# Attention scores from operands loaded early, two heads on two halves of the rows, sums by TensorE in the first 16 steps

## The chip, the cores and the metric

One Trainium2 chip, one of its cores. The metric is the device time of one execution in microseconds, the median of the runs. One execution was also taken with the hardware profiler; all rows below are from it.

## The reference

Three layers in a row, all float32. Attention: 4 batches, 8 heads, 576 positions, 64 dimensions a head.

```python
scores = scale * np.matmul(q, k.transpose(0, 1, 3, 2))        # scale = 1/8
bias = slopes[:, None, None] * (-np.abs(rel))[None, :, :]     # slopes 2^-(h+1), rel = pos_q - pos_k
mask = (rel >= 0) & (rel < 128)
scores = np.where(mask, scores + bias[None], -1e9)
attn = np.exp(scores - np.max(scores, axis=-1, keepdims=True))
attn = attn / (np.sum(attn, axis=-1, keepdims=True) + 1e-9)
x = np.matmul(attn, v)                                        # then (tokens 2304) x (512)
x = (np.maximum(x @ w_in, 0) ** 2) @ w_out                    # 512 -> 2048 -> 512
h = x @ w_in2; x = (h * np.cos(h)) @ w_out2                   # 512 -> 2048 -> 512
```

## The kernel before

**Tiling.** The 2304 tokens (the four batches, one behind the other) are 18 blocks `j` of 128 queries. A step `a` is one block and one of its four pairs of heads (`j, hp = divmod(a, 4)`; `e` is the head within the pair), so there are 72 steps. A query block needs its own keys and those of the block before it (`slot` says where each lies); the first block of each two batches needs only its own ("first"), block 4 of nine straddles two batches ("straddle", with a bias table of its own), the one behind it ("after") uses 192 columns.

**A step** is: `scores` (products of queries and keys into a PSUM bank, then for each head the bias and the row minimum of -score/8 in one VectorE instruction, line 386, and the exponential with its row sum on ScalarE, line 396), `normalise` (row sum plus 1e-9, reciprocal, and the scaling of the exponentials, lines 408, 409, 412), `transposes` (four TensorE transposes into a bank of `ps_s`, one ScalarE copy back, line 423) and `values` (products with V, line 449, of two heads into two halves of the columns; done for the four steps of a block together by `values_of_block`). With the fourth pair the block's output goes from PSUM to the next layer's operand as a high and a low part, `xh` (ScalarE, line 463) and `xl` (VectorE, line 464).

**Scores of the first seven blocks** (`PLAIN = 7`, steps 0 to 27) are full float32 products (line 354). Their operands are "planes" `s0_j` in the places of the weight tiles 9 to 15 (`S0`), 512 KB each in HBM: for each pair of heads, queries of head 0, a middle part with the keys of both heads, queries of head 1. The unused half of each query part is zeroed by POOL (lines 320, 321), so a product runs over all 128 rows and the zeros take the other head out. Later blocks use split operands (`QH`, `QL`, `KS`, line 365). A float32 product is two TensorE instructions in the trace.

**Two phases.** Steps 0 to 15 (`START = 16`) run ahead of the dense layers; their score banks are the four `ps_y` banks. Then the main loop runs over units of the dense layers (`h_mms`: 12 products of 512 columns, `y_mms`: 12 more), and one or two attention steps are put into each: scores of step s+1, `h_mms`, transposes of step s, `y_mms`. Their score banks come from `ps_s`, two banks, which the transposes use as well.

**Weights** come in 1 MB tiles, two loads ahead at most, and each is turned into a high and a low part by jobs (`w_top` ScalarE line 185 after a POOL memset, `w_rest` VectorE line 189, `w_split` ScalarE line 201 and VectorE line 204). `tick` advances the jobs. In the first phase two are started (`START_W`); tiles 9 to 15 wait for the planes in their places.

**Order.** Loads go to SP's queue (some of the first to ScalarE's) in written order: a load that waits for its buffer keeps those behind it waiting. `load_v(j + 2)` stands at the end of a block's values, and there are three V buffers; `load_plain(j + 2)` stands in `scores` of the block's second pair. On the other engines the framework makes one stream for each engine from the written order and its own estimate of when operands are ready, so conversions and steps interleave otherwise than they are written.

Of the kernel before, what the change touches and what calls it, by code (L numbers as in the profile page):

```python
# [8 lines left out]
F32 = mybir.dt.float32  # L9
F32R = mybir.dt.float32r  # L10
BF16 = mybir.dt.bfloat16
# [3 lines left out]
AF = mybir.ActivationFunctionType  # L15
ALU = mybir.AluOpType
# [6 lines left out]
P = 128  # L23
# [30 lines left out]

START, LOOK, PLAIN = 16, 2, 7


A_OPEN, W_OPEN, START_W = 20, 1, 2  # L60

SEAT = NF - PLAIN

# [10 lines left out]


@with_exitstack
def attention_mlp_mlp(ctx: ExitStack, tc: tile.TileContext, kq, s0, v, w1, w2, bias, strad, ident, out):

# [174 lines left out]
    def slot(j):  # L253

        return (j + j // 9) % 2
# [41 lines left out]
        )  # L297


    Pt, St, Tt, Oacc = {}, {}, {}, {}  # L300

    def kind(j):
        return {0: "first", 4: "straddle", 5: "after"}.get(j % 9, "plain")
# [2 lines left out]
        return {"first": (0, 128), "after": (64, 256)}.get(kind(j), (0, 256))  # L306

    def load_v(j, queue=sp):
        if j < NJ:
            V[j] = vp.tile([P, H * D], F32, tag="v", name=f"v_{j}")  # L310
            queue.dma_start(V[j], v[j])

    def load_plain(j, hps=slice(0, 4)):


        if j >= PLAIN:
            return
        t = plain(j)
        if hps.start == 0:
            pool.memset(t[64:128, :, 0], 0.0)  # L320
            pool.memset(t[0:64, :, 2], 0.0)
        for e in range(2):
            rows = slice(64 * e, 64 * e + 64)
            sp.dma_start(t[rows, hps, e : e + 2], s0[j][rows, hps])

    S0 = [wp.tile([P, 2048], F32, tag=f"w{SEAT + j}", name=f"s0_{j}") for j in range(PLAIN)]

    def plain(j):
        return S0[j][:, 0:1536].rearrange("p (a c t) -> p a c t", a=4, c=3)

    def scores_to(a):
        while now["qk"] < min(a, STEPS - 1):
            scores(now["qk"] + 1)

    def scores(a):

        j, hp = divmod(a, 4)
        if j >= PLAIN:
            if j == PLAIN:
                run_until(("kq", j - 1, hp))  # L340
            run_until(("kq", j, hp))
        now["qk"] = a
        if hp == 1:
            load_plain(j + 2)
            if j == 2:
                sp.dma_start(strad_sb, strad)
        if a < START:
            sbank = ps_y.tile([P, 2, 256], F32, tag=f"y{a % 4}", name=f"s_{a}")
# [13 lines left out]
        for i, src in enumerate((QH, QL)) if j >= PLAIN else ():  # L362
            for e in range(2):
                h = 2 * hp + e
                te.matmul(  # L365
                    sbank[:, e, :],
                    src[j, hp][:, e, :],
                    KS[:, :, h, :],
                    start=(i == 0 and e == 0),
                    stop=(i == 1),  # L370
                    skip_group_check=True,
                )
        if a < START:
            pt = S0[a % PLAIN][:, 1536:2048].rearrange("p (e c) -> p e c", e=2)
        else:
            pt = pp.tile([P, 2, 256], F32, tag="p", name=f"p_{a}")
        st = stp.tile([P, 8], F32, tag="st", name=f"st_{a}")
        Pt[a], St[a] = pt, st
        kd = kind(j)
        b0 = 0 if slot(j) else 128  # L380
        c0, c1 = cols(j)
        if kd == "after":
            pool.memset(pt[:, :, 0:64], 0.0)
        for e in range(2):
            h = 2 * hp + e
            dve.tensor_tensor_reduce(  # L386
                out=sbank[:, e, c0:c1],
                in0=sbank[:, e, c0:c1],
                in1=strad_sb[:, h] if kd == "straddle" else bias_sb[:, h, b0 + c0 : b0 + c1],
                scale=-0.125,  # L390
                scalar=3.0e38,
                op0=ALU.add,
                op1=ALU.min,
                accum_out=st[:, e : e + 1],
            )
            act.activation(  # L396
                pt[:, e, c0:c1],
                sbank[:, e, c0:c1],
                AF.Exp,
                bias=st[:, e : e + 1],  # L400
                scale=-1.0,
                accum_out=st[:, 2 + e : 3 + e],
            )
# [32 lines left out]
    def values(s):  # L436
        now["v"] = s
        j, hp = divmod(s, 4)
        ns = 1 if kind(j) == "first" else 2
        ptT = Tt.pop(s)  # L440
        if hp == 0:
            Oacc[0] = ps_o.tile([P, 4, P], F32, tag="o", name=f"o_{j}")
        ob = Oacc[0]
        for c in range(ns):

            blk = j if ns == 1 or c == slot(j) else j - 1
            for e in range(2):
                h = 2 * hp + e
                te.matmul(  # L449
                    ob[64 * e : 64 * e + 64, hp, :],  # L450
                    V[blk][:, h * D : h * D + D],
                    ptT[:, e, c, :],
                    start=(hp == 0 and c == 0),
                    stop=(c == ns - 1),
                    skip_group_check=True,
                )
# [148 lines left out]
    with ExitStack():  # L605
# [12 lines left out]
        dve.memset(halfpi, math.pi / 2)  # L618
        load_plain(0, slice(0, 1))
        act.dma_start(bias_sb[:, 0:2], bias[:, 0:2])  # L620
        load_plain(0, slice(1, 4))
# [136 lines left out]
```

## Time and profile before

| | |
|---|---|
| time, median of 3 runs | 936.79 us (935.21 to 937.61) |
| the profiled execution | 934.74 us, its span 933.0 us |
| mean granted TensorE clock | 0.996 of 2.4 GHz |
| busy: TensorE, VectorE, ScalarE | 911.6, 580.2, 502.8 us |
| moved by DMA | 70.36 MB |

The span runs from the first to the last instruction of the execution. An engine's busy time is what its instructions cover; the ends of TensorE's are modelled. In a timeline row with "x8", eight instructions are merged, and the first two numbers are the start and the length of the whole.

### The profile page before, as it was taken

The page shows a single profiled execution, that of the slowest core. Times are in us where ns is not written, and L with a number is a line of the kernel's source. Part 1 is how long each engine was busy: PE and PEld are TensorE (multiplying, and loading weights), DVE is VectorE, ACT ScalarE, POOL GpSimd, SP SyncE. Part 2 cuts the span into 40 slices and gives each one's busy share as a digit, 9 for nine tenths or more (in the row PEclk, how much of TensorE's full clock was granted, in tenths as well). Part 3 has the DMA queues.
Part 4 walks back from the last instruction along what each step waited for, and adds up shares of the span by engine and source line. Part 5 has one row for each costly group of instructions (what it writes and reads, how often), then busy time and mean ns, then how long its engine had stood idle before and what let it go on. Part 6 is the DMA issues. An engine that isn't in the chain of part 4 may idle for free.

```text
span 933.0 us, 13113 instructions
## 1 busy us (share of the span) xinstructions
PE 911.6 (98%) x5040; PEld 772.4 (83%) x5040; DVE 580.2 (62%) x1283; ACT 502.8 (54%) x1014; POOL 39.6 (4%) x58
## 2 busy tenths in 40 slices
PE   5699999999999999999999999999999999999998
PEld 5588888888888888888888888888888888888898
DVE  4969557666666566654645687566556555655554
ACT  5879656555555545554545575454444444444443
POOL 3112000000000000000110100000000000000000
PEclk9999999999999999999999999999999999999999
DMA  9773221311112111125234360011001000100010
GB/s 271 195 309 135 99 102 46 102 69 46 58 57 91 58 46 46 48 100 179 93 129 144 113 202 24 1 46 46 1 0 46 1 1 1 45 1 1 1 46 23
DMA packets 28846, 70.36 MB, mean 75 GB/s; under 512 B 2800, under 2 KB 11888, under 8 KB 28784
## 3 DMA queue, kind: packets, MB, share of 16 engines
q1 hardware_dynamic: 27920, 68.16, 21.8%
q10 hardware_dynamic: 864, 1.38, 0.6%
q8 instruction: 39, 0.64, 0.3%
q14 instruction: 23, 0.19, 0.1%
HBM read 60.09 MB, written 9.44 MB: 75 GB/s over the span
## 4 chain that ended last, share of the span: by engine, by line
PE 91%; ACT 4%; DVE 2%; DMA 2%; issue 1%; SPq 0%; POOL 0%; ACTq 0%; DVEq 0%
PE y L552 14%; PE y L554 13%; PE y L553 13%; PE h L493 13%; PE h L494 13%; PE h L495 13%; PE o L449 3%; PE t L421 3%; PE s L365 2%; PE s L354 2%; DMA s<-s_in 1%; ACT cv_w L185 1%; DVE cv_w L189 0%; ACT s L396 0%; ACT w L201 0%
## 5 line engine op out<-in xcount | busy, mean ns | idle before, releaser
L493 PE MATMUL h<-xh,w 128*128 128x512 f32 (+1 forms) x640 | 237.2, 371 | 0.0
L494 PE MATMUL h<-xl,w 128*128 128x512 f32 (+1 forms) x640 | 236.1, 369 | 0.0
L495 PE MATMUL h<-xh,w 128*128 128x512 f32 (+1 forms) x640 | 235.6, 368 | 0.0
L495 PEld LDWEIGHTS h<-xh,w 128*128 128x128 f32 x640 | 120.6, 188 | 20.4
L493 PEld LDWEIGHTS h<-xh,w 128*128 128x128 f32 x640 | 120.8, 189 | 19.4 <-ACT ysb L567 0.2
L494 PEld LDWEIGHTS h<-xl,w 128*128 128x128 f32 x640 | 120.9, 189 | 18.5
L552 PE MATMUL y<-rh,w 128*128 128x512 f32 (+1 forms) x320 | 123.4, 387 | 0.4 <-DVE ysb L567 0.4
L554 PE MATMUL y<-rh,w 128*128 128x512 f32 (+1 forms) x320 | 118.4, 370 | 0.0
L553 PE MATMUL y<-rl,w 128*128 128x512 f32 (+1 forms) x320 | 118.2, 370 | 0.0
L552 PE MATMUL y<-gh,w 128*128 128x512 f32 (+1 forms) x320 | 117.8, 369 | 0.2 <-ACT gh L532 0.2
L553 PE MATMUL y<-gl,w 128*128 128x512 f32 (+1 forms) x320 | 117.7, 368 | 0.0
L554 PE MATMUL y<-gh,w 128*128 128x512 f32 (+1 forms) x320 | 117.7, 368 | 0.0
L522 ACT ACTIVATE r<-r 128x512 f32<-128x512 f32 x72 | 45.5, 632 | 120.4 <-DVE r L521 120.4
L533 DVE TENSOR_TENSOR gl<-r,gh 128x512 fp32r<-128x512 f32 x72 | 49.8, 692 | 75.9 <-ACT gh L532 75.9
L519 DVE SCALAR_TENSOR_TENSOR r<-kk,h 128x512 f32<-128x512 int32 x72 | 49.5, 687 | 63.5 <-ACT kk L518 63.4
L510 DVE TENSOR_TENSOR a<-a 128x512 f32<-128x512 f32 x62 | 42.9, 692 | 62.9 <-ACT rh L509 59.9
L499 ACT ACTIVATE a<-h 128x512 f32<-128x512 f32 x72 | 43.0, 597 | 71.7 <-PE h L495 70.7
L396 ACT ACTIVATE p<-s,st 128x256 f32<-128x256 f32 (+2 forms) x112 | 51.5, 460 | 54.5 <-DVE st L386 54.4
L518 ACT ACTIVATE kk<-h 128x512 int32<-128x512 f32 x72 | 42.9, 596 | 69.3 <-PE h L495 69.2
L386 DVE CUSTOM_DVE_ANT_0 s<-s,bias_sb 128x256 f32<-128x256 f32 (+2 forms) x128 | 51.5, 407 | 38.6 <-PE s L354 13.9
L554 PEld LDWEIGHTS y<-rh,w 128*128 128x128 f32 x320 | 60.3, 188 | 10.7
L552 PEld LDWEIGHTS y<-rh,w 128*128 128x128 f32 x320 | 60.4, 189 | 10.4 <-issue 1.7
(69 smaller groups left out, 1377.0 us busy)
## 6 DMA issues: line engine op xcount, KB each, us to landing
raw<-w_in SPq DMA_DIRECT2D x32, 1023.8 KB, 6.9
raw_a<-kq_in SPq DMA_DIRECT2D x44, 256.0 KB, 2.6
y<-ysb SPq DMA_DIRECT2D x18, 256.0 KB, 2.1
raw_a<-y SPq DMA_DIRECT2D x18, 256.0 KB, 2.6
v<-v_in SPq DMA_DIRECT2D x16, 256.0 KB, 2.7
out<-ysb SPq DMA_DIRECT2D x16, 256.0 KB, 2.4
s<-s_in SPq DMA_DIRECT2D x12, 256.0 KB, 7.9
v<-v_in ACTq DMA_DIRECT2D x2, 256.0 KB, 6.5
```

Of the source, the lines that this page charges most:

```text
L386: dve.tensor_tensor_reduce(out=sbank[:, e, c0:c1], in0=sbank[:, e, c0:c1], in1=strad_sb[:, h] if kd == "straddle" else bias_sb[:, h, b0 + ...
L396: act.activation(pt[:, e, c0:c1], sbank[:, e, c0:c1], AF.Exp, bias=st[:, e : e + 1], scale=-1.0, accum_out=st[:, 2 + e : 3 + e],)
L493: te.matmul(o, wh[:, cs], xh, start=(c == 0 and kt == 0), stop=False, skip_group_check=True)
L494: te.matmul(o, wh[:, cs], xl, start=False, stop=False, skip_group_check=True)
L495: te.matmul(o, wl[:, cs], xh, start=False, stop=(kt == KT - 1), skip_group_check=True)
L499: act.activation(Aa[i], Hb.pop(i), AF.Relu)
L519: dve.scalar_tensor_tensor(r, kk, -C1, hb, ALU.mult, ALU.add)
L522: act.activation(r, r, AF.Abs)
L533: dve.tensor_tensor(rl, r, rh.bitcast(F32), ALU.subtract)
L552: te.matmul(o, wh, gh, start=(first and not (two and m % 2)), stop=False, skip_group_check=True)
L553: te.matmul(o, wh, gl, start=False, stop=False, skip_group_check=True)
L554: te.matmul(o, wl, gh, start=False, stop=last, skip_group_check=True)
```

## The change

Planes hold queries and keys of both heads of a pair, head 0 on rows 0 to 63 and head 1 on rows 64 to 127, with no zeros (1024 columns, one contiguous load for each plane). A score product runs over 64 rows, the two heads alternate, and each head has its own bank: in steps 0 to 15 two steps are made together and share two `ps_y` banks, in steps 16 to 27 one step takes half of both `ps_s` banks. The queues get all planes and V 0 to 2 ahead of the first step, with weight tiles 0 and 1 between them. One table of 640 bf16 columns is loaded in place of the bias tables (768 and 512 KB), and VectorE scales it for each head. In steps 0 to 15 the exponentials are not normalised and have no row sums: TensorE also multiplies the transposed exponentials with a tile of ones, into the `ps_h` bank, and the block's output is multiplied with the reciprocal of these sums. An exponential on a constant stands ahead of everything on ScalarE. Left out of the diff: the removed constants and argument, the packing of planes and tables on the host, and `kq` steps from 28 on, which stay as they were.

```diff
+    ones = cst.tile([P, D], F32, name="ones")
+    warm = cst.tile([P, 1], F32, name="warm")
+    dve.memset(halfpi, math.pi / 2)
+    dve.memset(ones, 1.0)
+    act.activation(warm, halfpi, AF.Exp)
...
     def top_up():
         for c in "aw":
-            if now["qk"] < {"a": A_OPEN, "w": W_OPEN}[c]:
+            if c == "a" and now["qk"] < A_OPEN:
...
     def load_v(j, queue=sp):
-        if j < NJ:
+        if j < NJ and j not in V:
...
-    def load_plain(j, hps=slice(0, 4)):
-        if j >= PLAIN:
-            return
-        t = plain(j)
-        if hps.start == 0:
-            pool.memset(t[64:128, :, 0], 0.0)
-            pool.memset(t[0:64, :, 2], 0.0)
-        for e in range(2):
-            rows = slice(64 * e, 64 * e + 64)
-            sp.dma_start(t[rows, hps, e : e + 2], s0[j][rows, hps])
+    def load_plain(j, hps=slice(0, 4), queue=sp):
+        queue.dma_start(plain(j)[:, :, hps], s0[j][:, :, hps])
...
+    def make_bias(dst, src, heads):
+        for h in heads:
+            dve.tensor_scalar(dst[:, h], src, 2.0**-h, None, ALU.mult)

     def scores_to(a):
         while now["qk"] < min(a, STEPS - 1):
-            scores(now["qk"] + 1)
+            a0 = now["qk"] + 1
+            steps = (a0, a0 + 1) if a0 < START else (a0,)
+            if a0 == START // 2:
+                make_bias(strad_sb, base_sb[:, 384:640], range(H))
+            scores(steps)
+            exps(steps)
...
+        if len(steps) == 2:
+            k = steps[0] // 2 % 2
+            banks = [ps_y.tile([P, 2, 256], F32, tag=f"y{2 * k + e}", name=f"s_{steps[0]}_{e}") for e in range(2)]
         else:
-            sbank = ps_s.tile([P, 2, 256], F32, tag="s", name=f"s_{a}")
-        if j < PLAIN:
-            for e in range(2):
-                for b in (j,) if kind(j) == "first" else (j, j - 1):
+            banks = [ps_s.tile([P, 2, 256], F32, tag="s", name=f"s_{steps[0]}_{e}") for e in range(2)]
+        for i, a in enumerate(steps):
+            Sc[a] = [bank[:, i] for bank in banks]
+            for b in (j,) if kind(j) == "first" else (j, j - 1):
+                for e in range(2):
+                    rows = slice(64 * e, 64 * e + 64)
                     te.matmul(
-                        sbank[:, e, slot(b) * P : slot(b) * P + P],
-                        plain(j)[:, hp, 2 * e],
-                        plain(b)[:, hp, 1],
-                        start=(e == 0 and b == j),
+                        Sc[a][e][:, slot(b) * P : slot(b) * P + P],
+                        plain(j)[rows, 0, a % 4],
+                        plain(b)[rows, 1, a % 4],
+                        start=(i == 0 and b == j),
...
+    def exps(steps):   # per head: the bias and row minimum of all steps, then their exponentials
...
+                    accum_out=St[a][:, 2 + e : 3 + e] if a >= START else None,
...   (values)
+            if s < START:
+                Oacc[1] = ps_h.tile([P, 4, P], F32, tag="h", name=f"sum_{j}")
...
+            products = [(ob, lambda h: V[blk][:, h * D : h * D + D])]
+            if s < START:
+                products.append((Oacc[1], lambda h: ones))
...
+            if s < START:
+                total = gp.tile([P, 4, P], F32, tag="a", name=f"total_{j}")
+                x = gp.tile([P, 4, P], F32, tag="a", name=f"x_{j}")
+                dve.tensor_scalar(total, Oacc[1], 1e-9, None, ALU.add)
+                dve.reciprocal(total, total)
+                dve.tensor_tensor(x, ob, total, ALU.mult)
+                ob = x
             act.copy(xh[:, :, ts], ob)
...
+        base_sb = rp.tile([P, 1024], BF16, tag="a", name="base_sb")
+        load_plain(0, slice(0, 2))
+        act.dma_start(base_sb[:, 0:640], bias)
+        make_bias(bias_sb, base_sb[:, 0:384], range(2))
+        load_plain(0, slice(2, 4))
         act.dma_start(id_sb, ident)
         load_v(0, act)
-        act.dma_start(bias_sb[:, 2:4], bias[:, 2:4])
-        act.dma_start(bias_sb[:, 4:8], bias[:, 4:8])
+        make_bias(bias_sb, base_sb[:, 0:384], range(2, H))
         load_plain(1)
-        load_v(1, act)
-
-        scores_to(0)
-        for s in range(START):
-            scores_to(min(s + LOOK, START))
+        AHEAD["w"] = 1
+        top_up()
+        load_plain(2)
+        load_v(1)
+        AHEAD["w"] = 2
+        top_up()
+        load_plain(3)
+        load_v(2)
+        for j in range(4, PLAIN):
+            load_plain(j)
+
+        scores_to(1)
+        for s in range(0, START, 2):
+            scores_to(min(s + 3, START))
             values_of_block()
-            normalise(s)
-            transposes(s)
-            tick("aw" if s < START_W else "a")
+            for a in (s, s + 1):
+                transposes(a)
+                tick("aw" if a < START_W else "a")
```

## Rows read from the trace of the kernel before

**Rows 1.** The page, busy time, share of the span and instructions of each engine.
```profile
PE 911.6 (98%) x5040; PEld 772.4 (83%) x5040; DVE 580.2 (62%) x1283; ACT 502.8 (54%) x1014; POOL 39.6 (4%) x58
```

**Rows 2.** Windows: length, busy time of each engine, granted clock, DMA share, GB/s.
```profile
0.00:5.20 5.20, 0.00 (x0) 0.02 (x1) 0.06 (x1) 0.00 (x0) 4.40 (x12) 1.00 0.57 159
5.20:9.90 4.70, 1.20 (x5) 0.95 (x5) 0.36 (x2) 1.74 (x3) 4.32 (x8) 1.00 1.08 224
9.90:41.60 31.70, 26.01 (x229) 22.52 (x229) 27.59 (x118) 27.74 (x77) 2.45 (x4) 1.00 0.89 250
41.60:46.30 4.70, 1.75 (x12) 1.14 (x12) 4.70 (x14) 2.97 (x11) 1.90 (x2) 0.70 0.89 202
46.30:53.50 7.20, 7.08 (x52) 6.00 (x53) 3.56 (x16) 3.28 (x8) 0.00 (x0) 0.72 0.36 124
53.50:132.50 79.00, 78.91 (x456) 66.13 (x454) 56.05 (x132) 59.33 (x119) 10.36 (x14) 1.00 0.42 157
```

**Rows 3.** The chain that ended last, 0 to 56 us: start, length, what.
```profile
2.65 7.11 DMA s<-s_in
...
41.64 0.53 SPq L324
42.22 4.13 DMA s<-s_in
```

**Rows 4.** Waits of SP's queue, 0 to 54 us: total, times, longest.
```profile
SPq L311 <- PE o L449: 24.6, 3, 9.7
```

**Rows 5.** Windows of lines 408, 409 and 412 alone: busy time, instructions.
```profile
0.00:53.50 53.50, 2.81 (x17) 0.94 0.80 218
0.00:53.50 53.50, 2.47 (x17) 0.94 0.80 218
0.00:53.50 53.50, 10.47 (x34) 0.94 0.80 218
```

**Rows 6.** Groups by form on VectorE: busy time, mean ns, idle before.
```profile
L521 DVE TENSOR_SCALAR r<-r 128x512 f32<-128x512 f32 x72 | 30.7, 426 | 2.1
...
L464 DVE TENSOR_TENSOR xl<-o,xh 128x512 fp32r<-128x512 f32 x18 | 12.4, 688 | 6.7 <-ACT xh L463 6.5
...
L409 DVE RECIPROCAL st<-st 128x2 f32<-128x2 f32 x72 | 11.6, 164 | 2.0
```

**Rows 7.** Timeline of ScalarE, two exponentials and a reading: start, length.
```profile
26.28 0.47 ACT L396 ACTIVATE s<-s,st 128x256 f32<-128x256 f32 x1
26.64 0.20 ACT L396 ACTIVATION_READ_ACCUMULATOR s<-s,st 128x1 f32 x1
26.73 0.47 ACT L396 ACTIVATE s<-s,st 128x256 f32<-128x256 f32 x1
```

**Rows 8.** A step's scores in the chain, a block's values in the timeline.
```profile
85.53 0.89 PE s L354 x8
...
81.67 2.28 PE L449 MATMUL o<-p,v 128*64 128x128 f32 x32
```

**Rows 9.** Groups by form, TensorE's weight loads of 128 and 64 columns.
```profile
L421 PEld LDWEIGHTS t<-id_sb,p 128*128 128x128 f32 x216 | 27.0, 140 | 7.1
L449 PEld LDWEIGHTS o<-p,v 128*64 128x64 f32 x432 | 23.3, 137 | 5.4 <-issue 5.1 <-ACT p L423 0.3
```

**Rows 10.** Timelines: three transposes and the next step's first exponential.
```profile
53.84 0.60 PE L421 MATMUL t<-id_sb,p 128*128 128x128 f32 x4
54.96 0.48 ACT L396 ACTIVATE p<-s,st 128x256 f32<-128x256 f32 x1
...
79.75 0.60 PE L421 MATMUL t<-id_sb,p 128*128 128x128 f32 x4
80.04 0.44 ACT L396 ACTIVATE p<-s,st 128x192 f32<-128x192 f32 x1
...
89.00 0.60 PE L421 MATMUL t<-id_sb,p 128*128 128x128 f32 x4
89.61 0.43 ACT L396 ACTIVATE p<-s,st 128x192 f32<-128x192 f32 x1
```

More of the change, by code (lines that the diff above doesn't have):

```diff
@@ L76, in attention_mlp_mlp @@
 @with_exitstack
-def attention_mlp_mlp(ctx: ExitStack, tc: tile.TileContext, kq, s0, v, w1, w2, bias, strad, ident, out):
+def attention_mlp_mlp(ctx: ExitStack, tc: tile.TileContext, kq, s0, v, w1, w2, bias, ident, out):
     nc = tc.nc
@@ L341, in scores @@
             run_until(("kq", j, hp))
[L342 to L348, printed above, removed]
-        else:
-            sbank = ps_s.tile([P, 2, 256], F32, tag="s", name=f"s_{a}")
-        if j < PLAIN:
-            for e in range(2):
-                for b in (j,) if kind(j) == "first" else (j, j - 1):
+            sbank = ps_s.tile([P, 2, 256], F32, tag="s", name=f"s_{a}")
+            Sc[a] = [sbank[:, e] for e in range(2)]
+            for i, src in enumerate((QH, QL)):
+                for e in range(2):
+                    te.matmul(
+                        Sc[a][e],
+                        src[j, hp][:, e, :],
+                        KS[:, :, 2 * hp + e, :],
+                        start=(i == 0 and e == 0),
+                        stop=(i == 1),
+                        skip_group_check=True,
+                    )
+            return
+        if len(steps) == 2:
+            k = steps[0] // 2 % 2
+            banks = [ps_y.tile([P, 2, 256], F32, tag=f"y{2 * k + e}", name=f"s_{steps[0]}_{e}") for e in range(2)]
+        else:
+            banks = [ps_s.tile([P, 2, 256], F32, tag="s", name=f"s_{steps[0]}_{e}") for e in range(2)]
+        for i, a in enumerate(steps):
+            Sc[a] = [bank[:, i] for bank in banks]
+            for b in (j,) if kind(j) == "first" else (j, j - 1):
+                for e in range(2):
+                    rows = slice(64 * e, 64 * e + 64)
                     te.matmul(
-                        sbank[:, e, slot(b) * P : slot(b) * P + P],
-                        plain(j)[:, hp, 2 * e],
-                        plain(b)[:, hp, 1],
-                        start=(e == 0 and b == j),
+                        Sc[a][e][:, slot(b) * P : slot(b) * P + P],
+                        plain(j)[rows, 0, a % 4],
+                        plain(b)[rows, 1, a % 4],
+                        start=(i == 0 and b == j),
                         stop=True,
@@ L361, in scores @@
                     )
[L362 to L378, printed above, removed]
+    def exps(steps):
+        j = steps[0] // 4
         kd = kind(j)
@@ L381, in scores @@
         c0, c1 = cols(j)
-        if kd == "after":
-            pool.memset(pt[:, :, 0:64], 0.0)
-        for e in range(2):
[L385 to L403, printed above, removed]
+        for a in steps:
+            if a < START:
+                k = a % (2 * PLAIN)
+                pt = S0[k // 2][:, 1024 + k % 2 * 512 : 1536 + k % 2 * 512].rearrange("p (e c) -> p e c", e=2)
+            else:
+                pt = pp.tile([P, 2, 256], F32, tag="p", name=f"p_{a}")
+            Pt[a], St[a] = pt, stp.tile([P, 8], F32, tag="st", name=f"st_{a}")
+            if kd == "after":
+                pool.memset(pt[:, :, 0:64], 0.0)
+        for e in range(2):
+            for a in steps:
+                h = 2 * (a % 4) + e
+                dve.tensor_tensor_reduce(
+                    out=Sc[a][e][:, c0:c1],
+                    in0=Sc[a][e][:, c0:c1],
+                    in1=strad_sb[:, h] if kd == "straddle" else bias_sb[:, h, b0 + c0 : b0 + c1],
+                    scale=-0.125,
+                    scalar=3.0e38,
+                    op0=ALU.add,
+                    op1=ALU.min,
+                    accum_out=St[a][:, e : e + 1],
+                )
+            for a in steps:
+                act.activation(
+                    Pt[a][:, e, c0:c1],
+                    Sc[a][e][:, c0:c1],
+                    AF.Exp,
+                    bias=St[a][:, e : e + 1],
+                    scale=-1.0,
+                    accum_out=St[a][:, 2 + e : 3 + e] if a >= START else None,
+                )
     def normalise(a):
@@ L446, in values @@
             blk = j if ns == 1 or c == slot(j) else j - 1
[L447 to L456, printed above, removed]
+            products = [(ob, lambda h: V[blk][:, h * D : h * D + D])]
+            if s < START:
+                products.append((Oacc[1], lambda h: ones))
+            for bank, stationary in products:
+                for e in range(2):
+                    te.matmul(
+                        bank[64 * e : 64 * e + 64, hp, :],
+                        stationary(2 * hp + e),
+                        ptT[:, e, c, :],
+                        start=(hp == 0 and c == 0),
+                        stop=(c == ns - 1),
+                        skip_group_check=True,
+                    )
         if hp == 3:
@@ L721, in bias_table @@
         c = np.arange(P)[None, :]
-        t = np.empty((P, H, 384), np.float32)
-        for h in range(H):
-            slope = 2.0 ** -(h + 1)
-            prev = np.where(c > r, -8.0 * slope * (P + r - c), -8.0e9)
-            cur = np.where(c <= r, -8.0 * slope * (r - c), -8.0e9)
-            t[:, h] = np.concatenate([prev, cur, prev], axis=1)
-        return t.astype(ml_dtypes.bfloat16)
-    def straddle_table():
-        t = bias_table()[:, :, 128:].copy()
-        t[64:, :, :64] = -8.0e9
-        t[64:, :, 128:] = -8.0e9
-        return t
+        out = -8.0e9 * 2.0 ** (H - 1)
+        prev = np.where(c > r, -4.0 * (P + r - c), out)
+        cur = np.where(c <= r, -4.0 * (r - c), out)
+        ends = np.where((r >= 64) & (c < 64), out, cur), np.where(r >= 64, out, prev)
+        return np.concatenate([prev, cur, prev, *ends], axis=1).astype(ml_dtypes.bfloat16)
     arrays = {
```

25 lines of the change are left out of this document (11 added, 14 removed).

## Prediction

> **What bounds the kernel now.** I read the page's busy shares first. TensorE is busy 98% of the span [rows 1], so a gain can only come from its 2% of gaps or from TensorE work that goes away. The busy times by stretch show where the gaps are [rows 2]: from 53.5 to 132.5 us TensorE is busy 78.91 of 79.00 us, so everything behind 53.5 us is bound by TensorE's own work. Ahead of 53.5 us it isn't. Of 5.2 to 9.9 us TensorE works 1.20 us and VectorE 0.36. From 9.9 to 41.6 us three engines are nearly level: ScalarE 27.74, VectorE 27.59, TensorE 26.01 of 31.70 us. From 41.6 to 46.3 us TensorE works 1.75 of 4.70 us. In the two stretches from 41.6 to 53.5 us the granted clock averages 0.70 and 0.72, so about half of each ran at 1.2 GHz and not at 2.4: it fell after TensorE had begun to stand.
>
> The chain of waits names the two holes [rows 3]. The first is the load of the rest of plane 0, in flight from 2.65 to 9.76 us. The second is the load of plane 4: SP issues it only at 41.64 us and TensorE waits for it until 46.35. The waits of SP's queue say why it is issued late [rows 4]: the load of V blocks (line 311) waits 24.6 us in three waits, up to 9.7 us each, for the value products that free its buffer, and plane 4's load stands behind one of them.
>
> **Early loads.** All seven planes and V 0 to 2 go to the queues ahead of the first step, before any load that waits for a buffer, so the 41.6 us hole has no cause left. That is worth up to 4.7 us. VectorE was busy through the whole hole [rows 2], but partly with conversions of weight tiles 2 and 3, which can go behind 53.5 us, where VectorE is idle 79.0 - 56.05 = 23 us; I take 3.5. The cold stretch behind it (46.3 to 53.5 us) held TensorE 7.08 us at a mean clock of 0.72; at the full clock the same work is about 7.08 x 0.72 = 5.1 us, 2.0 less. Together -5.5 us (bounds -2, if VectorE binds there after all, and -6.7). What is late next is the load of V 3, which waits for V 0's buffer and is needed in block 3 only. In SP's queue weight tile 0 now stands between planes 1 and 2, and tile 1 between 2 and 3; the 1.0 MB of tile 0 and the 0.52 MB each of planes 1 and 2 are, at the 250 GB/s of [rows 2], 2.1 MB or 8.4 us behind plane 0, so about 15 us, when block 2 is not yet on; all of it (planes, tiles 0 and 1, V 1 and 2: 5.7 MB) is there 23 us behind plane 0, at about 29 us, and step 16 needs plane 4 at about 40.
>
> At the start 5.2 us x 159 GB/s + 4.7 us x 224 GB/s = 1.9 MB had come in when the rest of plane 0 was there [rows 2]. Now steps 0 to 3 need plane 0 (0.52 MB), a table of 0.16 MB in place of 0.77 MB of bias, the identity (0.07) and V 0 (0.26): 1.0 MB, which those rates bring by 5.2 + (1.0 - 0.83) / 0.224 = 6.0 us. So the hole shrinks from 4.7 us to about 1.2: -3.5 us (bounds 0, if the table, which now leaves ScalarE's queue behind the warm-up exponential, is as late as plane 0 was; and -4.7). The memsets of the planes on POOL go; they were ahead of need.
>
> **VectorE and ScalarE in the first 16 steps.** The normalising by rows (lines 408, 409, 412) cost 2.81 + 2.47 + 10.47 = 15.75 us for 17 steps [rows 5]; step 16 keeps it, so 14.8 go. Added for each of four blocks are a sum with 1e-9, a reciprocal and a product, each 128x512. The sum and the product read PSUM like the xl subtraction, 0.69 us [rows 6]. No 128x512 reciprocal is in the trace: one pass like the scalar operation of that shape is 0.43 us; the 128x2 form took 0.164 us, at most 82 ns a column if nothing of it were fixed, which gives 42 us for 512. Between ends so far apart I take the nearest 128x512 row, 0.69; the range keeps 0.43 and, above, eight passes (4.4, among the rivals), and leaves 42 out. So 4 x 2.07 = 8.3 us come. The tables cost 16 scalings of 384 or 256 columns; by the 512-column row at most 0.43 us each, at least 0.16 like the 2-column one; I take 0.3, 4.8 us. VectorE: -14.8 + 8.3 + 4.8 = -1.7 us. ScalarE loses the reading of the row sums: an exponential takes 0.36 us from its start to the reading's, and 0.09 more until the next one starts [rows 7]: 32 x 0.09 = -2.9 us.
>
> The Trainium skill, "VectorE: DVE Perf Modes", section "First, the fixed hardware budget", says that a reciprocal runs iterative divide operations with a repeat count of 8. The two-column row cannot show it; by that rule the sum here would be 9 us worse, which is the second rival below.
>
> **TensorE in the first 16 steps.** Scores cost 0.89 us a step of two blocks [rows 8], so eight instructions of 0.111 us. Two heads on different halves of the rows are not in the trace. The nearest row is the value products, which stand on two halves of the columns: 32 in 2.28 us, 0.071 each [rows 8]. Bounds are 0.111 (no overlap; a little above that if switching costs) and half of it, 0.055. I take 0.071, so 0.57 a step, and 0.32 saved. For 4 half steps and 12 whole ones that is 14 x 0.32 = -4.5 us. The sums by TensorE double the value products: 4 x 0.29 + 12 x 0.57 = +8.0 us. TensorE's net is +3.5 us.
>
> In the stretch from 9.9 to 41.6 us this makes TensorE 29.5, VectorE 26 and ScalarE 25 of 31.7 us: two engines lighter, the third heavier but below the length. I take 0 for its length (bounds -3, as ScalarE's saving, and +5, TensorE's extra work and the dependences of pairs). At the end of the phase the sum, the reciprocal and the product stand in a row ahead of xh: 3 x 0.69 = 2.1 us, which only the scores and transposes of steps 16 and 17 can cover: +1.5 us (0 to +2.1).
>
> The Trainium skill, "TensorE: Matmul & The Clock Gate", section "LDWEIGHTS (loading the stationary operand)", says that a weight load takes as long as it has columns, however few rows. The trace agrees on columns [rows 9]: 23.3 / 432 = 0.054 us busy per load of 64 columns, 27.0 / 216 = 0.125 of 128. If loads alone set the pace, scores gain nothing; that is the third rival. The same page's "Measured speedup vs the span model" has row tiles run side by side, by which they would halve.
>
> **Behind the first phase.** Steps 17 to 27 also take their scores from the planes: 11 x 0.30 (0.32 less a switch in and out) = -3.3 us (0 to -5). But each such step now takes both banks of ps_s, one for each head, and the transposes use the same two. So a transpose that stands on TensorE waits until the first exponential of the next step has freed its bank; y products are queued behind it, and ScalarE's copy waits for it. Laid on the trace of before [rows 10], the transposes at 53.84, 79.75 and 89.00 us would wait for exponentials that end at 54.96 + 0.48 = 55.44, 80.48 and 90.04: 1.6 + 0.7 + 1.0 = 3.3 us; in the other eight steps the exponential ends in time. The engines' order can differ around the first, so I take +2.5 (0 to +6).
>
> **Sum.** -5.5 - 3.5 + 0 + 1.5 - 3.3 + 2.5 = -8.3 us. The profiled execution took 934.74 us (933.0 of span), so 926.4; the median of the runs, 936.79, is 2.05 above it, so I forecast 928.5 us.
>
> **Rivals.**
> The transposes bind (0.10): with the phase shorter, the backlog of weight conversions on ScalarE and VectorE (59.33 and 56.05 of 79 us, [rows 2]) moves on to steps 17 to 27, and every first exponential is late. Without its term the forecast is 926.0, so 939.6 us is reached at 13.6 us of waiting, 13.6 / 11 = 1.2 us a step; the three rows have 0.7 to 1.6. At 1.4 a step it is 926.0 + 15.4 = 941 us, slower. Against it: eight of eleven are in time.
> The divide is slow (0.15): if each column costs eight passes, a reciprocal is 8 x (0.69 - 0.16) + 0.16 = 4.4 us, 3.7 more. Three of them make VectorE 26 + 11 = 37 us in a stretch of 31.7, +5.3, and the last is fully exposed, +3.7: 937.5 us. For it stands nothing in the rows; against it only that two columns take 0.164 us in all.
> Heads side by side don't overlap (0.18), the part of the change that then doesn't do what it says: 3.3 us are lost behind the phase, and TensorE in the stretch has 26.0 + 8.0 = 34, which with the gaps makes 35.5 in place of 31.7: 928.5 + 3.3 + 3.8 = 935.6 us. The wide loads of [rows 9] speak for it, the value products' pace against it.
> The forecast has 0.57; its own range is 922 to 934.
>
> A difference within 0.3% (2.8 us) can't be told from none: faster is below 934.0, slower above 939.6. Faster: 0.56 of the forecast, 0.03 of the slow divide, 0.07 of the third rival: 0.66. Slower: the transposes 0.10, 0.03 from the other two: 0.13. The rest, 0.21, is no change. The range reaches down to 919 (bounds of the start, the stretch and the scores) and up to 938 (the slow divide).
>
> **What would show it.** Right: no TensorE gap over 1 us between 12 us and the first h product, the clock full up to there, and that product at about 45 to 48 us, not 53.5; score instructions at about 0.07 us; the reciprocal at about 0.7 us. Wrong: the reciprocal above 2 us with VectorE filled between 10 and 45 us; score instructions still 0.11 us apart; TensorE waiting for exponentials ahead of transposes by more than 1.2 us a step between 50 and 130 us; or a new wait for the table ahead of the first step.

## The result

The changed kernel takes 945.81 us (median of 4 runs, 944.35 to 947.17) against 937.2 for the kernel before: ratio 1.0094, interval 1.0078 to 1.0109. It is slower; 928.5 was forecast. Its profiled execution took 946.89 us (span 944.8), 12.1 us more than that of before; the lags below are between these two. The page's busy times (against [rows 1]):

```profile
PE 924.6 (98%) x5152; PEld 776.4 (82%) x5152; DVE 588.3 (62%) x1248; ACT 500.5 (53%) x983; POOL 32.2 (3%) x44
```

TensorE has 112 more instructions (the ones products) and 13 us more busy time. The busy times by stretch, with the columns of [rows 2]:

```profile
0.00:5.20 5.20, 1.03 (x8) 0.93 (x8) 1.87 (x12) 1.49 (x2) 2.04 (x6) 1.00 0.64 202
5.20:9.90 4.70, 3.46 (x16) 2.21 (x15) 2.97 (x22) 2.48 (x9) 0.00 (x0) 1.00 0.96 390
9.90:41.60 31.70, 29.95 (x299) 25.19 (x298) 24.88 (x62) 22.36 (x44) 1.90 (x2) 0.89 0.66 265
41.60:46.30 4.70, 2.97 (x27) 2.07 (x24) 4.70 (x5) 2.16 (x4) 0.00 (x0) 1.00 1.01 377
46.30:53.50 7.20, 6.53 (x60) 5.20 (x60) 5.05 (x10) 5.89 (x10) 1.91 (x2) 0.76 0.55 229
53.50:65.00 11.50, 6.46 (x24) 4.76 (x21) 11.30 (x20) 5.91 (x13) 0.49 (x1) 0.68 0.86 315
```

The start gave what was forecast: TensorE has done 4.5 us of work by 9.9 us, not 1.2. In the long stretch the three engines stand at 29.95, 24.88 and 22.36 us, against 29.5, 26 and 25 forecast. But these are not the loads of the whole stage: TensorE's clock is at half for 6.8 us of the stretch (0.89 on average), and at 41.6 us it has started 320 of the 409 instructions that stand ahead of its first h product. The stage is not over at 53.5 us either: from there to 65 TensorE is busy 6.46 of 11.50 us. The chain that ended last shows what fills that time (start, length, what), against [rows 3]:

```profile
53.44 0.24 PE sum L473 x4
53.70 0.69 DVE total L491
...
54.79 3.21 DVE total L492
...
58.38 0.54 DVE x L493
58.92 0.27 DVE p L431
...
59.33 0.45 PE t L440
59.78 0.65 PE h L525
...
62.94 0.43 PE h L527
```

The plane load of [rows 3] is gone from the chain. In its place stands the last division: sum, reciprocal, product, 53.70 to 58.92 us, and behind it on VectorE the normalising of step 16 (L431), for which TensorE's transposes wait 5.0 us. TensorE's clock falls while it stands, and the first h products run 0.43 us apart, where 0.23 is the pace at the full clock. The windows around that (third last column: granted clock):

```profile
53.50:57.60 4.10, 0.79 (x8) 0.52 (x4) 3.90 (x4) 1.51 (x5) 0.00 (x0) 1.00 0.76 214
57.60:67.80 10.20, 8.47 (x23) 6.10 (x24) 7.99 (x17) 4.96 (x10) 1.91 (x2) 0.50 0.67 274
```

So the first h product starts at 59.6 us (in the chain it is counted from 59.78, when the transpose ahead of it is done) instead of 53.5, and the first y product 10.5 us later than before. From there to the 192nd y product the lag stays at 10.4; 1.3 us more are lost at about 190 us. The division's instructions on VectorE until 66 us, and the tables' (line, engine, operation, shapes, count, busy us, mean ns), against [rows 5, 6]:

```profile
L492 DVE RECIPROCAL total<-total 128x512 f32<-128x512 f32 x4 | 13.4, 3350 | 0.1
...
L491 DVE TENSOR_SCALAR total<-sum 128x512 f32<-128x512 f32 x4 | 2.7, 687 | 2.7 <-PE sum L473 2.7
...
L493 DVE TENSOR_TENSOR x<-o,total 128x512 f32<-128x512 f32 x4 | 2.7, 684 | 0.0
...
L331 DVE TENSOR_SCALAR bias_sb<-base_sb 128x384 bf16<-128x384 bf16 x8 | 1.4, 254 | 2.1 <-DMA base_sb<-bias_in 2.1
L331 DVE TENSOR_SCALAR strad_sb<-base_sb 128x256 bf16<-128x256 bf16 x8 | 1.3, 220 | 0.0
```

One reciprocal of 512 columns takes 3.35 us, 4.9 times the 0.687 of the sum, which reads PSUM, and 7.0 times the 0.480 that a scaling of the same tile takes in e1 below. The waits of SP's queue, against [rows 4], and what TensorE waited for until 80 us (total, times, longest), against [rows 10]:

```profile
SPq L317 <- PE o L473: 22.2, 2, 11.6
SPq L317 <- PE sum L473: 12.6, 1, 12.6
```
```profile
PE s L376 <- DMA s<-s_in: 5.4, 3, 4.2
PE t L440 <- DVE p L431: 5.0, 1, 5.0
PE t L440 <- ACT p L415: 1.9, 1, 1.9
```

The V loads still wait for buffers, but no wait of TensorE's for one shows. Transposes wait 1.9 us once for an exponential. A step's scores among steps 17 to 27 (timeline: start, length), against [rows 8]:

```profile
79.08 0.39 PE L585 MATMUL y<-rl,w 128*128 128x512 f32 x1
79.31 0.39 PE L586 MATMUL y<-rh,w 128*128 128x512 f32 x1
79.63 0.49 PE L376 MATMUL s<-s 64*128 64x128 f32 x4
79.95 0.39 PE L376 MATMUL s<-s,s 64*128 64x128 f32 x4
80.27 0.50 PE L525 MATMUL h<-xh,w 128*128 128x512 f32 x1
80.61 0.39 PE L526 MATMUL h<-xl,w 128*128 128x512 f32 x1
```

Eight products of two heads start within 0.64 us, not 0.89. But the y ahead of them takes 0.32 us to its successor and the h behind them 0.34, where 0.23 is usual (79.08 to 79.31).

### The profile page after: what moved, and what is told of

Its sections match the earlier page's. It is cut to its first block, busy times and chain, and to the rows that moved or that the text cites. A ratio compares the mean times of both kernels' runs of the same rounds, so it can differ in the third digit from the quotient of the medians.

```text
span 944.8 us, 13215 instructions
## 1 busy us (share of the span) xinstructions
PE 924.6 (98%) x5152; PEld 776.4 (82%) x5152; DVE 588.3 (62%) x1248; ACT 500.5 (53%) x983; POOL 32.2 (3%) x44
## 4 chain that ended last, share of the span: by engine, by line
PE 89%; DVE 5%; ACT 2%; issue 2%; DMA 1%; SPq 0%; POOL 0%; DVEq 0%; ACTq 0%
PE y L584 13%; PE h L525 13%; PE y L586 13%; PE y L585 13%; PE h L526 13%; PE h L527 13%; PE t L440 3%; PE o L473 3%; PE s L357 2%; PE s L376 1%; DVE w L210 1%; DVE cv_w L195 1%; DMA raw_a<-kq_in 1%; ACT cv_w L191 1%; DMA s<-s_in 1%
```

## Experiments

Times are medians, each uncertain by 1 to 2 us by its interval. The kernel before took 936.5 to 936.6 us beside the first twelve, 937.2 beside the last three and the changed kernel; where that matters ratios are compared, times 936.6.

**Which part costs.** Four kernels, one edit each: division made cheap, old normalising brought back, and each half of the change alone.

```diff
 # e1
-                dve.reciprocal(total, total)
+                dve.tensor_scalar(total, total, 1.0, None, ALU.mult)
 # e2: without total, x and the ones products; row sums read again
             for a in (s, s + 1):
+                normalise(a)
                 transposes(a)
 # e3: before, with the order of loads of the change (planes in the old layout)
-            if now["qk"] < {"a": A_OPEN, "w": W_OPEN}[c]:
+            if c == "a" and now["qk"] < A_OPEN:
 # e4: before, with ones products and division by blocks, no normalise(s)
+                products.append((Oacc[1], lambda h: ones))
```

> The changed kernel with the four 128x512 reciprocals replaced by a scaling of the same shape (0.43 us as in the trace of before); the division is left out. Theory A (the reciprocal, 3.35 us each in the changed kernel, is the cost: three of them hold up VectorE, the fourth leaves TensorE standing 5 us and cold for 8 us behind it): first h product at about 48 us in place of 59.6, no stretch at 1.2 GHz behind it, and 929 to 934 us in all. Rival B (the added products with ones and the pairs of steps bind the first phase): TensorE's work in the phase is as before, first h product at 55 to 58 us, 940 to 944 us. Rival C (the shared banks cost it behind the phase): 943 us or more.

Measured 939.24 us (ratio to before 1.003, 1.0016 to 1.0044).

> The changed kernel with the exponentials normalised by rows again (row sums on ScalarE, 128x2 reciprocals and the scaling on VectorE) and without the products with ones: the early loads, the tables made on chip and the two halves of the rows stay. Theory A: the rest of the change is worth what was forecast for it, first h product at about 46 to 48 us, 925 to 931 us. Rival B: the same or a little less, since the products with ones go too. Rival C: the banks of steps 16 to 27 keep it at 937 us or more.

Measured 936.79 (1.0006, 0.9989 to 1.0022).

> The kernel before with one edit: all planes (in the old layout, with their zeros), V 0 to 2 and weight tiles 0 and 1 are issued ahead of the first step, the straddle table behind them. Theory: the hole at 41.6 us and the cold stretch behind it go, 5.5 us by the forecast's own term, 930 to 933 us; the first hole stays, as the bias table is loaded as before. Rival (the loads only move the wait, as VectorE was busy through the hole anyway): 935 to 938 us.

Measured 936.64 (1.0003, 0.9988 to 1.0017).

> The kernel before with one edit: in the first 16 steps no normalising by rows, but the sums by products with ones and the division of a block's output, with the 128x512 reciprocal. Theory A: VectorE loses 14.8 us and gains 4 x (3 x 0.69 + 2.66) = 19 us, the last block's 4.7 us are exposed and the clock falls behind them: 942 to 950 us. Rival B' (VectorE has room for it, and the loss in the changed kernel comes of the pairs and the loads): 936 to 939 us.

Measured 947.09 (1.0112, 1.0083 to 1.0141).

e1 lies between theory A (929 to 934 us) and rival B (940 to 944), with its first h product at 55.6 us, where B had it. e2 missed theory A; its number is rival C's, but e9 below has the same banks and 928.6, so the banks are not the reason.

So the reciprocal is worth 945.8 - 939.2 = 6.6 us by the medians ((1.0094 - 1.0030) x 936.6 = 6.0 by the ratios), and all of the slowing belongs to sums and division: alone they cost before 10.5 us. And what was to give 8 to 10 us, loads, halves and tables, gives nothing where rows are normalised (e2).

**Why the rest gives nothing.** Two suspects: TensorE's order and VectorE's work. In e2 the products of one head follow each other (timeline):

```profile
17.12 0.38 PE L376 MATMUL s<-s,s 64*128 64x128 f32 x2
17.34 0.38 PE L376 MATMUL s<-s 64*128 64x128 f32 x2
```

Two start in 0.22 us, 0.11 each: no overlap. I take it that head 0's bank comes free first and its products for both steps go ahead; the trace does not name the head. e5 and e6 order them alternately; e8 and e9 normalise nothing.

```diff
 # e5 (on e2), e6 (on the change), e8 (on e9)
-                for e in range(2):
+                for e in (1, 0):
...
+                    if chain:
+                        tc.add_manual_dep(mm, chain[-1].name, NOSYNC, reason="heads alternate")
+                    chain.append(mm)
 # e9 (on e2)
-                normalise(a)
+                St.pop(a)
```

> The changed kernel normalising by rows (as in e2_rows_normalised, 936.8 us), and in the first 16 steps TensorE's score products are put in the order head 1, head 0, head 1, head 0 instead of one head's for both steps first. Theory T (the order of TensorE sets the first stage: products of one head follow each other at 0.112 us, and those of alternating heads in pairs at 0.105 us): some 50 of the 120 products are saved at 0.05 to 0.11 us each, first h 3 to 5 us earlier, 930 to 934 us. Theory V (VectorE's stream of bias, row maximum and normalising sets the stage): no change, 936 to 938 us.

Measured 935.51 (0.9982, 0.9966 to 0.9997).

> e2_rows_normalised without any normalising in the first 16 steps (sum with 1e-9, reciprocal and product by rows are left out there, so the values of blocks 0 to 3 stay unscaled). VectorE loses some 14.8 us of work and each step its wait between exponential and transposes. Theory V (VectorE's stream sets the first stage): 928 to 931 us, first h 5 us or more earlier. Theory T (TensorE's order and its changes between scores, transposes and values set it): 935 to 937 us.

Measured 928.60 (0.9906, 0.9887 to 0.9924).

> The changed kernel as it is (945.8 us, with ones products and the division by blocks), with the heads of the score products alternating as in e5_heads_alternate. Theory T: 940 to 943 us. Theory D (the chain bank, sum, reciprocal, product, copy, first products of the stretch ends the stage, and what is ahead of it only waits): 944 to 946 us.

Measured 943.46 (1.0061, 1.0047 to 1.0075).

> e9_no_normalise with the heads alternating. Where VectorE alone sets the stage: as e9 within 1 us. Where TensorE's order sets it: 3 to 5 us below e9. Where both bind in turn: below e5 and below e9 by more than either alone gives against e2, 925 to 928 us.

Measured 928.61 (0.9903, 0.9888 to 0.9917).

Theory V holds in the main: normalising by rows costs 936.8 - 928.6 = 8.2 us, and with it gone the order is worth nothing. The readings of the row sums on ScalarE go with it (2.9 us of ScalarE by the forecast) and are in the 8.2. The order alone gives 1.3 us (e5; by the ratios 2.2) and 2.3 (e6; 3.1): both runs came out between the two theories, below the 3 to 5 us of theory T.

**The sums' price, and the other corner of the square.** e10 keeps the ones products without a division, e13 is before without normalising; e11 and e12 try to make normalising cheaper.

```diff
 # e10 (on the change): total, x and their three operations go
+                seen = stp.tile([P, 8], F32, tag="seen", name=f"seen_{j}")
+                dve.tensor_copy(seen, Oacc[1][:, 3, 0:8])
 # e11 (on e5), all steps
-        dve.tensor_scalar(st[:, 4:6], st[:, 2:4], 1e-9, None, ALU.add)
-        dve.reciprocal(st[:, 6:8], st[:, 4:6])
+        dve.reciprocal(st[:, 6:8], st[:, 2:4])
 # e12 (on e11), first 16 steps, in place of the products by rows
+                pool.tensor_scalar(Dg[0][:, a % 2 * 2 + e], id_sb, st[:, 6 + e : 7 + e], None, ALU.mult)
+                    te.matmul(tb[:, e, c, :], pt[:, e, c * P : c * P + P], Dg[0][:, s % 2 * 2 + e], start=True, stop=True)
 # e13 (on before; as in e9 and e14, no row sums are read either)
-            normalise(s)
+            St.pop(s)
```

> The changed kernel with the ones products but no division by blocks at all (values of blocks 0 to 3 stay unscaled; VectorE only reads 8 columns of the sums' bank, so that the bank is waited for as before). Beside e9_no_normalise (928.6 us) it adds the ones products alone; beside e1_no_divide (939.2 us) it leaves out 4 times three one-pass operations of some 0.69 us. If TensorE's own time is what the sums cost: 936 to 937 us (928.6 and 7.7 of products). If VectorE sets the stage and the products lie under it: 929 to 931 us, and e1's one-pass operations are then the dearer part.

Measured 934.59 (0.9978, 0.9963 to 0.9993).

> e5_heads_alternate (935.5 us) without the sum with 1e-9 ahead of the reciprocal by rows, in all steps: the row's sum holds an exp(0) = 1, so that in float32 the sum does not change. One VectorE instruction of 0.25 us and its hand-over go from each of the first 16 steps. Theory V (VectorE's stream sets the first stage): 16 x 0.25 = 4 us off VectorE, 930 to 933 us. Theory T (TensorE's order sets it, once the heads alternate): 934 to 936 us.

Measured 930.46 (0.9930, 0.9911 to 0.9950).

> e11_alternate_no_add, and in the first 16 steps the two products by rows (2 x 0.35 us of VectorE a step) go: GpSimd multiplies the identity by the reciprocals instead (two instructions of 128x128 a step), and the transposes become products with that diagonal matrix. Theory V: some 16 x 0.69 = 11 us off VectorE, less what the wait for GpSimd takes: 926 to 930 us. Rival: GpSimd's two instructions (no row of before shows their price; its memset of 128x128 took 0.22 us) and one more hand-over between engines lengthen each step's chain: 932 us or more.

Measured 939.89 (1.0028, 1.0015 to 1.0042).

> The kernel before with nothing normalised in the first 16 steps (sum, reciprocal and product by rows left out, values of blocks 0 to 3 unscaled). It is the fourth corner of a square with before (936.5), e2_rows_normalised (936.8) and e9_no_normalise (928.6). If the early loads, halves and chip-made tables are covered by VectorE's work: here, where that work is gone too, the late transfers bind, and it takes 933 to 936 us. If these edits are worth nothing by themselves, and normalising costs the same on both sides: 928 to 930 us.

Measured 930.11 (0.9934, 0.9912 to 0.9956).

The ones products cost 934.6 - 928.6 = 6.0 us, of 7.7 us of TensorE work: not under VectorE, as theory V alone would have it (929 to 931), and not all of it. The three one-pass operations of e1 then cost 939.2 - 934.6 = 4.6. The clock is in these prices: in the profiled executions TensorE runs 3.4 us at half speed in e10, 13.7 in e1 and 20.5 in the changed kernel (up to 90 us), and no run parts work from clock. Dropping one small sum per step, here in all 72 steps, gives 5.0 us on e5, of which 3.8 are there at the first h product: e11 beats both kernels, and VectorE's work alone was touched. e12 fell for a reason the traces show (groups on GpSimd and TensorE):

```profile
L441 POOL TENSOR_SCALAR diag<-id_sb,st 128x128 f32<-128x128 f32 x32 | 25.6, 819 | 16.3 <-DVE st L436 15.2 <-PE t L455 1.1
```
```profile
L455 PE MATMUL t<-diag,s 128*128 128x128 f32 x112 | 19.7, 333 | 2.5 <-POOL diag L441 2.4
```

GpSimd takes 0.82 us for 128x128, and a float32 product is two instructions where a transpose is one: 112 for 56 tiles.

Without normalising, loads, halves and tables together give 930.1 - 928.6 = 1.5 us (2.6 by the ratios), which the intervals do not keep clear of nothing. The last three runs take that apart.

```diff
 # e14 (on e3)
-            normalise(s)
+            St.pop(s)
 # e15 (on before), all steps
-        dve.reciprocal(st[:, 6:8], st[:, 4:6])
+        dve.reciprocal(st[:, 6:8], st[:, 2:4])
 # e16 (on e2, with e11's reciprocal): planes padded with zeros as before
-                        plain(j)[rows, 0, a % 4],
-                        plain(b)[rows, 1, a % 4],
+                        plain(j)[:, a % 4, 2 * e],
+                        plain(b)[:, a % 4, 1],
```

> e3_early_loads_alone (the kernel before with the early plane, value and weight loads only) with nothing normalised in the first 16 steps, as e13_before_no_normalise (930.1 us). If the early loads pay once VectorE's work is out of their way: 926 to 928 us, as far below e13 as e9_no_normalise (928.6) or more, and halves and chip-made tables are then worth nothing or cost. If they are worth nothing even here: 929.5 to 931 us, and the 1.5 us between e13 and e9 belong to halves and tables.

Measured 934.20 (0.9971, 0.9959 to 0.9983).

> The kernel before without the sum with 1e-9 ahead of the reciprocal by rows, in all steps (as e11_alternate_no_add, 930.5 us). If VectorE's stream sets the first stage of before as well: 16 x 0.25 us and their hand-overs go, 931 to 934 us. If the hole until the second plane sets it: 936 us.

Measured 933.86 (0.9968, 0.9956 to 0.9981).

> e2_rows_normalised without the sum with 1e-9 (as e11) and with the score products of the first 28 steps back at 128 rows: planes with zeros in the other head's rows, cleared by GpSimd, as in before; early loads, tables made on chip and steps in pairs stay. Beside e11_alternate_no_add (930.5 us) it undoes the halves alone. If a product of a half at 0.053 us against one of 0.112 is worth what it says: 8 us or more of TensorE come back in the first 28 steps, 935 us or more. If the changes of tile shape around each group of halves (0.2 us each way) take the gain: 929 to 932 us.

Measured 936.82 (0.9994, 0.9983 to 1.0005).

e14 missed both expectations: early loads alone, with the old planes, cost (0.9971 - 0.9934) x 936.6 = 3.5 us against e13. What TensorE waited for until 60 us, in e13, e14, e9 and e16 (the longest waits, and for e14 and e16 the next):

```profile
PE s L354 <- POOL cv_w L183: 5.1, 1, 5.1
PE s L354 <- DMA s<-s_in: 3.6, 1, 3.6
```
```profile
PE s L350 <- DMA s<-s_in: 8.3, 2, 5.2
...
PE t L417 <- DVE p L408: 2.6, 1, 2.6
```
```profile
PE s L376 <- DMA s<-s_in: 6.4, 2, 4.3
```
```profile
PE s L381 <- POOL s L324: 5.9, 1, 5.9
...
PE t L444 <- DVE s L435: 5.0, 3, 4.1
```

The waits in the first lines (8.7, 8.3, 6.4 and 5.9 us) all lie ahead of 10 us. (e13's first one is put down to a memset for a weight tile, which the product does not read; in before and in e14 the same product waits for the plane's load, until 5.2 us.) Between e13 and e14 the early loads took 0.4 us off them. The hole of plane 4 is in none of the four: in e13, with the loads in the old order, TensorE works on through the stretch of the hole at the full clock:

```profile
41.60:46.30 4.70, 4.16 (x45) 3.12 (x44) 2.58 (x7) 3.17 (x9) 0.95 (x1) 1.00 0.01 4
```

So with the normalising gone early loads had no hole left to close. e14 loses there instead: TensorE waits 2.6 us for the normalising of step 16, which ends at 44.8 us, and soon behind it runs at half the clock for 6.8 us. Why the normalising comes so late in e14 is not shown.

e16 undoes the halves at a cost of (0.9994 - 0.9930) x 936.6 = 6.0 us against e11 (which also alternates the heads), but little of that is the products' pace. In e16 GpSimd clears planes until 8.8 us and places for weights until 10.5, and VectorE scales the tables meanwhile:

```profile
L337 DVE TENSOR_SCALAR bias_sb<-base_sb 128x384 bf16<-128x384 bf16 x8 | 4.5, 634 | 2.2 <-DMA base_sb<-bias_in 2.2
L337 DVE TENSOR_SCALAR strad_sb<-base_sb 128x256 bf16<-128x256 bf16 x8 | 3.7, 846 | 0.0
```

The same scalings take 254 and 220 ns in the changed kernel, which clears no planes. The chain that ended last runs through them in e16: the first normalised tile of e16 is late, TensorE waits 4.1 us for it (last row of the waits above), and its clock is at half for the 6.8 us from 12.6. I added, over TensorE's instructions up to the first h, the time from each start to the next (gaps above 0.45 us counted as idle, above 0.6 where the clock is low). From e16 to e11 the first h comes 6.27 us earlier: 1.63 by an earlier first product (half the plane's transfers, no clearing), 1.90 by less idle time, 2.74 by TensorE's work. Of the last, some 1.7 is 3.4 us less time at half the clock (10.24 against 6.83), and some 0.9 is four score instructions and four transposes that stand ahead of the first h in e16 alone. So next to nothing is left for the products' pace. The cleaner pair is e13 and e9; with time at half the clock counted half, TensorE's work up to the first h is 32.3 and 31.6 us: scores 17.2 to 15.1, transposes 7.6 to 8.6, values 7.4 to 7.9. Their timelines (full rows, then halves) show where the gain goes:

```profile
20.19 0.60 PE L421 MATMUL t<-id_sb,s 128*128 128x128 f32 x4
20.62 0.39 PE L354 MATMUL s<-s 128*128 128x128 f32 x2
...
21.30 0.39 PE L354 MATMUL s<-s,s 128*128 128x128 f32 x2
21.52 0.60 PE L421 MATMUL t<-id_sb,s 128*128 128x128 f32 x4
```
```profile
21.29 0.65 PE L440 MATMUL t<-id_sb,s 128*128 128x128 f32 x4
21.87 0.37 PE L376 MATMUL s<-s,s 64*128 64x128 f32 x1
21.88 0.37 PE L376 MATMUL s<-s 64*128 64x128 f32 x1
22.09 0.27 PE L376 MATMUL s<-s,s 64*128 64x128 f32 x1
...
24.91 0.39 PE L376 MATMUL s<-s,s 64*128 64x128 f32 x4
25.14 0.39 PE L376 MATMUL s<-s 64*128 64x128 f32 x4
```

With full rows, transposes and scores follow each other without a step: four in 0.43 us, eight in 0.90. With halves, the four transposes take 0.58 to the first score and the first pair 0.21; in the run, four products take 0.23 (24.91 to 25.14). The saving of 0.44 us on eight products meets about 0.25 us at the way in and some more at the way out, as behind 79.95 us above.

## Why the prediction was wrong

In a chain of runs, each one step from the last: 936.5 before; 930.1 without normalising (e13); 928.6 with the loads, halves and tables (e9); 934.6 with the ones products (e10); 939.2 with three one-pass operations a block (e1); 945.8 with a true reciprocal.

- **The step that failed: "I take 0 for its length".** The stretch was to keep its length because each engine's sum stayed below it. The sums to 41.6 us came near (29.95, 24.88 and 22.36 us), but the stage was not over, and no engine's room kept its work out of the time: ones products on TensorE (8.0 us forecast, 7.7 measured) came back as 6.0 us, normalising by rows, mostly VectorE's, as 6.5 to 8.2. The bound of +5 named there was the nearer one. With it the largest single term was mis-sized, the divide.
- **The divide** was taken at 0.69 us and took 3.35 (rival 2: 4.4). It cost 6.0 to 6.6 us; that rival had put 9 on it. The Trainium skill, "VectorE: DVE Perf Modes", "First, the fixed hardware budget", has the divide repeated 8 times. The rows come near that against a scaling of the same tile in SBUF (3.35 to 0.480 us in e1, 7.0 times), and not against the sum that reads PSUM (4.9 times), which the forecast had taken. Even without a true divide e1 took 939.2, 2.6 us more than before: the divide was the largest term, not the only one.
- **The normalising by rows** was costed as 14.8 us of VectorE and gave 6.5 (e13) to 8.2 us (e9). Sum and product by blocks: with the scaling in place of the divide, 7.3 us of VectorE were 4.6 of time, the clock's share included.
- **Early loads, -5.5.** Nothing came of them: e3 gives 0.0, less than even the bound of -2 "if VectorE binds there after all", and e14 costs 3.5. The hole was over-read. In before TensorE does not stand for all of the 4.7 us, and not only for the plane; its waits between 41.6 and 46.4 us are

```profile
PE o L449 <- DVE xl L464: 1.7, 1, 1.7
...
PE t L421 <- DMA s<-s_in: 1.3, 1, 1.3
```

  and e13 has no hole there though its loads come in the old order. In e3 the hole is gone (TensorE is busy 4.25 us from 41.6 to 46.3), but TensorE stands behind it: it is busy 5.51 of 7.20 us to 53.5 and 14.81 of 16.50 to 70 (7.08 and 16.50 in before). That VectorE's small instructions count in before itself e15 shows: 0.17 us less VectorE work a step, in all 72 steps, gives 3.0 us ((1 - 0.9968) x 936.6).
- **The cold clock, -2.** Before runs 6.8 us at half speed behind the hole, the changed kernel 20.5 us in three stretches: 6.8 from 30.6 us, 3.4 from 47 and 10.2 behind the last division. By the rows the last alone is 8.47 x 0.5 = 4.2 us of the 10.5; no run of the changed kernel kept the clock up. Where it stayed up, in seven of the ten executions of e3 (mean granted clock 1.000), the median was 936.5 all the same.
- **The start, -3.5.** It came (4.5 us of work by 9.9 us in place of 1.2) and was lost in the stage: without normalising, start, halves and tables together give 1.5 us.
- **Tail, +1.5.** It was 53.70 to 58.92, 5.2 us, and not covered by steps 16 and 17, since step 16's normalising stands behind the division in VectorE's queue (58.92 us, behind the product at 58.38).
- **Scores, 0.071 us each.** Alternating heads do better, 0.105 a pair; but part of the first stage ran as in e2, 0.11 each, and each change of shape costs about 0.1 us on both sides. So the 4.5 us forecast for 16 steps were some 2 for the scores, and transposes and values took most of that back (e13 and e9). Rival 3 (heads don't overlap) was true in part, for a reason that it did not name. The Trainium skill, "TensorE: Matmul & The Clock Gate", "Measured speedup vs the span model", has row tiles run side by side; pairs at 0.105 agree. Weight loads did not limit them: two loads of 128 columns went in 0.105 us.
- **Steps 17 to 27, -3.3.** The lag is 10.5 us at the first y and 10.4 at the 192nd: 0.1 gained. By the timeline 0.25 is saved a step and 0.20 lost at the two changes of shape.
- **Bank wait, +2.5.** One wait of 1.9 us ahead of 80 us, and none above 0.4 from there to 135; rival 1 did not happen.
- **Tables, 0.3 each.** 0.254 and 0.220.

Open: why step 16's normalising comes late in e14; how much of each price is the clock's; and the 1.3 us lost at about 190 us in the changed kernel, where TensorE waits 1.7 us for a VectorE copy of y (0.4 in before).

## What to carry over

Where three engines hand work to each other step by step, judge an edit by taking it out of the stage and not by whether its engine has room: an instruction of about 0.2 us in each step's chain, dropped from all 72, was worth 3 to 5 us, a 5 us hole in the loads nothing. Read such a hole by TensorE's own waits in it, and not by the one transfer that ends it. Price a reciprocal by its columns, and keep it on the narrow side (2 columns a step and not 512 a block). A product on half the rows is quicker when the heads alternate and many stand together; count two changes of shape for each group, which left a gain of 0.7 us in 16 steps here.

## What was not expected of the hardware

- A float32 reciprocal of 128x512 takes 3.35 us on VectorE, 6.5 ns a column; one of 128x2 0.16 us.
- Float32 products of two heads on two halves of the rows start in pairs 0.007 us apart, a pair every 0.105 us, where they alternate; in e2, where they seem not to, one takes 0.11 us.
- A change between 64-row and 128-row products costs 0.09 to 0.15 us (y to scores 0.32 in place of 0.23, scores to h 0.34, transposes to scores 0.58 in place of 0.43), with no wait in the trace.
- GpSimd takes 0.82 us to scale a 128x128 float32 tile; VectorE's form of that size took 0.28 in e2.
- VectorE's bf16 scalings of 384 columns took 0.63 us each while GpSimd cleared planes (e16), and 0.25 in the changed kernel, where GpSimd cleared none.
